# Loading and preparing the first pair's V ahead of the other pairs in a fused attention and mixer kernel

## The chip, the core and the metric

The kernel runs on one core of a Trainium2 chip. The metric is device time in microseconds (us). The engines are PE (TensorE, the matrix engine; PEld is its weight load), DVE (VectorE), ACT (ScalarE), POOL (GpSimd) and SP (SyncE, which here issues every DMA).

## The reference

```python
scores = scale * np.matmul(q, k.transpose(0, 1, 3, 2))     # batch 2, heads 12, seq 448, head_dim 64
scores = np.where(mask, -1000000000.0, scores)              # causal
attn = softmax(scores); x = np.matmul(attn, v)              # x: 2 x 448 x 768
xt = x.transpose(0, 2, 1)
u = x + (np.maximum(xt @ w_tok1, 0.0) @ w_tok2).transpose(0, 2, 1)   # token mixing, 448 -> 256 -> 448
y = u + np.maximum(u @ w_ch1, 0.0) @ w_ch2                  # channel mixing, 768 -> 1536 -> 768
h = gelu(y @ w_in)                                          # 768 -> 1024, halves u and v
gated = u * (w_sg applied over tokens to layernorm(v) + b_sg)
out = y + gated @ w_out                                     # 512 -> 768
```

The weights of the two mixing layers come as 64-bit floats. Products are kept near 32-bit accuracy by splitting each operand into a high and a low part and adding three matmuls.

## The kernel before

**Attention** runs over 24 heads in 12 pairs of two heads (`pair`, `order`). For a pair, `prep_qk` loads k (one DMA, 224 KB) and q (two DMAs), and `prep_v` loads V (one DMA, 320 KB, tile `vr`) and prepares it: the largest absolute value of each row on DVE (`am`, L255), a matmul that spreads it over the partitions (`vm`, L257), three short DVE operations that make the scale `sv` (L259 to L261), then the high half `vh` on ACT (L262) and the low half `vl` on DVE (L263). Each head has two halves, so a pair has four half-steps, 48 in all. A half-step (`probabilities`) makes scores on PE (L286, tile `s`), masks them and takes the row minimum on DVE (L291), takes the exponential on ACT (L298), rounds to a 16-bit high part on ACT (L300, `hl`), subtracts for the low part on POOL (L301) and transposes both parts with one DMA (L303, `pT<-hl`, "transpose" below; they are numbered 1 to 48 in order). `values` then multiplies the transposed probabilities with `vh` and `vl` on PE (L326 to L328, into `x_ps`, one buffer), and DVE scales the result of a pair (L342 to L344, `xf`). POOL and ACT split it into `xh` and `xl`.

**Token mixing** (`token_mix`) follows after every second pair: matmuls `a_ps` with w_tok1 (L361, L362, L136 to L138), a ReLU on ACT (`ah`, L366), matmuls `u_ps` with w_tok2 (L377) and the residual.

**Channel mixing** is the dense part: `channel_up` (`r_ps`, L136 to L138, 18 matmuls of 448 columns for one weight tile and one batch), then `channel_down` (`y_ps`). Each weight tile is loaded as 64-bit words (`wraw`, 768 KB, two buffers) and converted on ACT (`wm`, L113), DVE (L116, L117), ACT (`whi`, L121) and POOL (`wlo`, L94). Seven `channel_up` groups of the first batch (`NF0`, `up`) are written so that they may stand among the attention of the second batch. The gated layer (`v_ps`, `ug_ps`, `g_ps`, `o_ps`) ends the kernel.

**What sets the order.** The kernel is written in plain program order, and a scheduler that runs when the program is built orders the instructions of each engine, taking earlier written work first, unless a block gives another priority. `prepare_v` puts `prep_v` in such a block. On the chip each engine, and SP's queue of DMA issues, works through its own list in that fixed order. So a change of what is written first can move instructions anywhere in the attention.

Of the kernel before, what the change touches and what calls it, by code (L numbers as in the profile page):

```python
# [27 lines left out]
def mixer_kernel(  # L28
# [32 lines left out]
    AHEAD = 4  # L61
    VAHEAD = 2
# [133 lines left out]
    with ExitStack() as at:  # L196
# [42 lines left out]
        def prep_qk(b, n):  # L239

            qp = qps[n % len(qps)]
            k2 = qkp.tile([P, S], F32, tag="k2", name="k2")
            nc.sync.dma_start(k2, k[b, n])
            for i in range(2):
                nc.sync.dma_start(qp[i * D:(i + 1) * D, i * S:(i + 1) * S], q[b, n, i * D:(i + 1) * D])
            return qp, k2

        def prep_v(b, n):

            vr = qkp.tile([P, NVC, 2 * D], F32, tag="vr", name="vr", bufs=2)  # L250
            nc.sync.dma_start(vr, v[b, n])
            hi, lo = vts[n % NVT]
            vr4 = vr.rearrange("p c (h d) -> p c h d", h=2)
            am = stp.tile([P, 1], BF16, tag="am", name="am")
            nc.vector.tensor_reduce(am, vr[:, 1:5], AX.XY, ALU.max, apply_absolute_value=True)  # L255
            pm = ps_e.tile([P, 512], F32, tag="d", name="vm")
            nc.tensor.matmul(pm[:, :P], am.to_broadcast([P, P]), ident_b, start=True, stop=True)  # L257
            sv = stp.tile([P, 1], F32, tag="sv", name="sv")
            nc.vector.reduce_max(sv, pm[:, :P], axis=AX.X)  # L259
            nc.vector.tensor_scalar(sv, sv, 1e-20, 1.0 / VSCALE, ALU.max, ALU.mult)  # L260
            nc.vector.reciprocal(sv, sv)  # L261
            nc.scalar.activation(hi[:, :, :, :D], vr4, AF.Copy, scale=sv[:, 0:1])  # L262
            nc.vector.scalar_tensor_tensor(lo, vr4, sv[:, 0:1], hi[:, :, :, :D], ALU.mult, ALU.subtract)  # L263
            return hi, lo, sv
# [129 lines left out]
        qks, vss = {}, {}  # L394

        def prepare(n):
            if n < len(order):
                b, h = order[n]
                if h % 2 == 0:
                    qks[b, h // 2] = prep_qk(b, h // 2)  # L400

        def prepare_v(n):
            if n < len(order) and n % 2 == 0:
                b, h = order[n]

                with tc.high_priority(offset=-80):
                    vss[b, h // 2] = prep_v(b, h // 2)
# [6 lines left out]
            with tc.issue_after(marks[H - 2 + m]):  # L414
                channel_up(m, [0], rpool, ps_e)

        for n in range(AHEAD):
            prepare(n)
        for n in range(VAHEAD):
            prepare_v(n)  # L420
        for n, (b, h) in enumerate(order):
            prepare(n + AHEAD)
# [196 lines left out]
```

## Time and profile before

| | us |
|---|---|
| median of 3 runs | 428.05 (427.13 to 430.08) |
| the profiled execution's own time | 429.13 |
| its span, first to last instruction | 427.3 |
| PE busy in the span | 399.9 (94%) |
| PE idle in the span (the difference) | 27.4 |
[...]

The span is 1.8 us shorter than that execution's own time. Busy shares are averages over stages: attention ends near 170 us, and the dense part follows.

### The profile page before, as it was taken

To read this page: it belongs to the slowest core of one execution; us is meant where nothing else is said; L and a number is where in the kernel's file an instruction comes from. 1 tells how busy PE (TensorE), PEld (TensorE's weight loads), DVE (VectorE), ACT (ScalarE), POOL (GpSimd) and SP (SyncE) were. 2 spreads that over 40 slices of the span, in tenths; PEclk is the share of its full clock that TensorE was granted. 3 is DMA by queue.
4 is the path that set the end of the run, shared out by engine and by line. 5 is a ranking of instruction groups with operands and counts; after the bars stand their busy time and mean duration, and the time that the engine had idled before them with its cause. 6 is when DMAs were issued, how large, how long until landed. Compare 5 with 4: busy or idle time off the path is not lost.

```text
span 427.3 us, 6998 instructions
## 1 busy us (share of the span) xinstructions
PE 399.9 (94%) x2567; PEld 340.3 (80%) x2567; DVE 238.4 (56%) x522; ACT 204.2 (48%) x389; POOL 246.5 (58%) x234
## 2 busy tenths in 40 slices
PE   5878788888998999999999999999999999999996
PEld 3545666776787998999999999999998889965995
DVE  5989566787693645344444275557437451249422
ACT  3888678697665454445344244334423232332100
POOL 2789768769777564464335247454556653225662
PEclk9989999999898999999999999999999999999999
DMA  7999999999987854446344344453354001100122
GB/s 213 199 290 235 209 173 208 252 220 265 242 170 164 163 160 154 137 156 220 123 132 157 106 127 144 134 181 110 126 163 135 0 0 51 49 2 0 76 98 86
DMA packets 66738, 62.29 MB, mean 146 GB/s; under 512 B 53136, under 2 KB 58384, under 8 KB 66704
## 3 DMA queue, kind: packets, MB, share of 16 engines
q1 hardware_dynamic: 66704, 61.85, 56.5%
q8 instruction: 20, 0.33, 0.3%
q14 instruction: 14, 0.11, 0.1%
HBM read 46.50 MB, written 2.75 MB: 115 GB/s over the span
## 4 chain that ended last, share of the span: by engine, by line
PE 67%; DMA 12%; POOL 8%; ACT 5%; SPq 2%; issue 2%; DVE 2%; POOLq 0%; ACTq 0%; DVEq 0%
DMA pT<-hl 8%; PE y_ps L137 7%; PE y_ps L136 7%; PE y_ps L138 7%; PE r_ps L138 6%; PE r_ps L136 6%; PE r_ps L137 6%; POOL hl L301 4%; DMA vr<-in 2%; PE v_ps L138 2%; PE o_ps L136 2%; PE o_ps L138 2%; PE o_ps L137 2%; PE ug_ps L136 2%; PE v_ps L137 2%; PE ug_ps L138 2%
## 5 line engine op out<-in xcount | busy, mean ns | idle before, releaser
L94 POOL TENSOR_TENSOR wlo<-wm,whi 128x768 fp32r<-128x768 f32 (+1 forms) x41 | 81.3, 1984 | 75.6 <-ACT whi L121 75.1
L116 DVE TENSOR_SCALAR wm<-wm 128x768 int32<-128x768 int32 (+2 forms) x53 | 34.1, 643 | 88.0 <-ACT wm L113 88.0
L301 POOL TENSOR_TENSOR hl<-pe,hl 128x512 f16<-128x512 f32 x48 | 60.5, 1267 | 29.2 <-ACT hl L300 25.2
L113 ACT ACTIVATE wm<-wraw 128x768 f32<-128x768 f32 (+2 forms) x53 | 42.7, 805 | 59.1 <-POOL wlo L94 47.7
L286 PE MATMUL s_ps<-k,q 128*128 128x64 f32 (+3 forms) x216 | 57.9, 410 | 8.3 <-DMA q<-in 4.6
L138 PE MATMUL r_ps<-u_hi,wlo 128*128 128x448 f32 x144 | 53.4, 370 | 0.0
L137 PE MATMUL r_ps<-u_lo,whi 128*128 128x448 f32 x144 | 53.2, 369 | 0.0
L136 PE MATMUL r_ps<-u_hi,whi 128*128 128x448 f32 x144 | 53.1, 369 | 0.0
L136 PE MATMUL y_ps<-rh,whi 128*128 128x448 f32 x144 | 52.6, 365 | 0.0
L138 PE MATMUL y_ps<-rh,wlo 128*128 128x448 f32 x144 | 52.6, 365 | 0.0
L137 PE MATMUL y_ps<-rl,whi 128*128 128x448 f32 x144 | 52.6, 365 | 0.0
L121 ACT CAST whi<-wm 128x768 fp32r<-128x768 f32 (+1 forms) x41 | 32.8, 800 | 37.8 <-PE ug_ps L137 11.6
L117 DVE SCALAR_TENSOR_TENSOR wm<-wraw,wm 128x768 int32<-128x768 int32 (+2 forms) x53 | 50.1, 945 | 1.0
L286 PEld LDWEIGHTS s_ps<-k,q 128*128 128x128 f32 x216 | 32.4, 208 | 17.2 <-issue 6.6
L298 ACT ACTIVATE pe<-pe,bias 128x192 f32<-128x192 f32 (+3 forms) x84 | 40.2, 522 | 0.4
L291 DVE CUSTOM_DVE_ANT_0 pe<-s_ps,mask 128x320 f32<-128x320 f32 (+3 forms) x84 | 34.6, 444 | 7.9 <-PE s_ps L286 6.1
L300 ACT CAST hl<-pe 128x512 f16<-128x512 f32 x48 | 29.3, 612 | 18.3 <-DMA pT<-hl 17.9
L326 PE MATMUL x_ps<-vh,pT 128*128 128x65 f16 (+1 forms) x240 | 26.3, 197 | 11.6 <-DMA pT<-hl 10.9
L326 PEld LDWEIGHTS <-pT 128*128 128x128 f16 (+1 forms) x240 | 21.2, 98 | 19.6 <-DMA pT<-hl 14.6
L94 POOL TENSOR_TENSOR u_lo<-yt,u_hi 128x448 fp32r<-128x448 f32 x12 | 13.9, 1156 | 30.1 <-ACT u_hi L193 30.1
L138 PEld LDWEIGHTS r_ps<-u_hi,wlo 128*128 128x128 f32 x144 | 27.2, 189 | 2.6 <-issue 0.4
L136 PEld LDWEIGHTS r_ps<-u_hi,whi 128*128 128x128 f32 x144 | 27.3, 189 | 2.4 <-issue 0.2
(140 smaller groups left out, 918.7 us busy)
## 6 DMA issues: line engine op xcount, KB each, us to landing
wraw<-in SPq DMA_DIRECT2D x35, 768.0 KB, 4.5
wraw<-in SPq DMA_DIRECT2D x14, 512.0 KB, 3.9
vr<-in SPq DMA_DIRECT2D x12, 320.0 KB, 3.8
k<-in SPq DMA_DIRECT2D x12, 224.0 KB, 3.4
q<-in SPq DMA_DIRECT2D x24, 112.0 KB, 3.4
out<-ob SPq DMA_DIRECT2D x12, 224.0 KB, 1.9
wraw<-in SPq DMA_DIRECT2D x3, 256.0 KB, 3.1
pT<-hl SPq DMA_TRANSPOSE x48, 4.4
```

The costliest lines, as they stand in the source:

```text
L94: nc.gpsimd.tensor_sub(lo, src, f32(hi))
L113: nc.scalar.activation(m, words.bitcast(F32)[:, :, 1], AF.Prelu, scale=2.0 ** -112, alpha=-(2.0 ** 32))
L116: nc.vector.tensor_scalar(mi, mi, 3, None, ALU.logical_shift_left)
L117: nc.vector.scalar_tensor_tensor(mi, words[:, :, 0], 29, mi, ALU.logical_shift_right, ALU.bitwise_or)
L136: nc.tensor.matmul(ps, lh, rh, start=i == 0 and not begun, stop=False)
L137: nc.tensor.matmul(ps, lh, rl, start=False, stop=False)
L138: nc.tensor.matmul(ps, ll, rh, start=False, stop=i == n - 1)
L286: nc.tensor.matmul(ps[:, o:o + m], qp[:, q0:q0 + P], k2[:, ks], start=True, stop=True)
L291: nc.vector.tensor_tensor_reduce(out=pe[:, cs], in0=ps[:, cs], in1=mask0 if i == 0 else mask[:, MASKS[i]], scale=-1.0 / math.sqrt(D), scal ...
L298: nc.scalar.activation(pe[:, cs], pe[:, cs], AF.Exp, bias=bias[:, j:j + 1], scale=-1.0)
L301: nc.gpsimd.tensor_sub(hl[:, 1], pe, hl[:, 0])
L326: nc.tensor.matmul(o, ph, vh[:, c, h, :D + 1], start=j == 0, stop=False)
```

## The change

Before, the q and k of the first two pairs are requested first (`AHEAD` is 4 heads), and then the V of the first pair, in the block with the other priority. With the change the order is q and k of the first pair, V of the first pair, q and k of the second pair, and the first pair's `prep_v` is called directly, outside that block, before any scores are written. Nothing is added or taken away.

```diff
-        for n in range(AHEAD):
+
+        prepare(0)
+        vss[0, 0] = prep_v(0, 0)
+        for n in range(1, AHEAD):
             prepare(n)
-        for n in range(VAHEAD):
+        for n in range(1, VAHEAD):
             prepare_v(n)
```

Because the scheduler works from the program order, the lists of all engines differ through the whole attention. From the last token mixing on they are alike again. Three places:

**DVE at the start**, from the first score mask (`pe_194`) on. `am_163` before and `am_159` in the change are the first pair's V, `am_179` is the second pair's; `mx` rows belong to the mask above them. Before:

```order
L291 ISA pe_194,mx_195<-s_ps_193,mask0_76 128x64
L291 ISA mx_195 128x1
L291 ISA pe_194,mx_195<-s_ps_193,mask_77 128x448
L291 ISA mx_195 128x1
L291 ISA pe_228,mx_229<-s_ps_227,mask_77 128x192
L291 ISA mx_229 128x1
L291 ISA pe_228,mx_229<-s_ps_227,mask_77 128x320
L291 ISA mx_229 128x1
L255 TENSOR_REDUCE am_163<-vr_161 128x1
L291 ISA pe0_126,mx0_128<-s_ps_259,mask_77 128x448
L291 ISA mx0_128 128x1
L255 TENSOR_REDUCE am_179<-vr_177 128x1
```

With the change:

```order
L255 TENSOR_REDUCE am_159<-vr_157 128x1
L291 ISA pe_194,mx_195<-s_ps_193,mask0_76 128x64
L291 ISA mx_195 128x1
L291 ISA pe_194,mx_195<-s_ps_193,mask_77 128x448
L291 ISA mx_195 128x1
L291 ISA pe_228,mx_229<-s_ps_227,mask_77 128x192
L291 ISA mx_229 128x1
L291 ISA pe_228,mx_229<-s_ps_227,mask_77 128x320
L291 ISA mx_229 128x1
L259 TENSOR_REDUCE sv_163<-vm_161 128x1
L255 TENSOR_REDUCE am_179<-vr_177 128x1
L291 ISA pe0_126,mx0_128<-s_ps_259,mask_77 128x448
```

The first pair's `am` moves from behind four masks to ahead of the first, and the second pair's `am` from behind the mask of the third half-step (`pe0_126`) to ahead of it.

**SP's queue at the same time**; `pT_242`, `pT_268`, `pT_297` are transposes 2, 3 and 4, `vr_328` is the third pair's V, which reuses the first pair's `vr` buffer, and `wraw` is a token-mixing weight. Before:

```order
L303 DMA_TRANSPOSE pT_242<-hl_239 128x8x128
L105 DMA wraw_424<-in_3 128x256
L303 DMA_TRANSPOSE pT_268<-hl_265 128x8x128
L303 DMA_TRANSPOSE pT_297<-hl_294 128x8x128
L105 DMA wraw_432<-in_3 128x256
L251 DMA vr_328<-in_2 128x640
L243 DMA k2_574<-in_1 128x448
```

With the change:

```order
L303 DMA_TRANSPOSE pT_242<-hl_239 128x8x128
L105 DMA wraw_424<-in_3 128x256
L105 DMA wraw_432<-in_3 128x256
L245 DMA q1_135<-in_0 64x448
L251 DMA vr_328<-in_2 128x640
L303 DMA_TRANSPOSE pT_268<-hl_265 128x8x128
L243 DMA k2_574<-in_1 128x448
L303 DMA_TRANSPOSE pT_297<-hl_294 128x8x128
```

Transposes 3 and 4 stood ahead of `vr_328` and stand behind it now, and behind one more weight and a q load.

**SP's queue around transpose 41** (`pT_2012`); `pT_1873` and `pT_1902` are 39 and 40, and `wraw_2481`, `wraw_2514`, `wraw_2572` are the 6th, 7th and 8th channel-mixing weight tiles. Before:

```order
L105 DMA wraw_2481<-in_5 128x768
L303 DMA_TRANSPOSE pT_1873<-hl_1870 128x8x128
L303 DMA_TRANSPOSE pT_1902<-hl_1899 128x8x128
L105 DMA wraw_2514<-in_5 128x768
L105 DMA wraw_2572<-in_5 128x768
L303 DMA_TRANSPOSE pT_2012<-hl_2009 128x8x128
L303 DMA_TRANSPOSE pT_2047<-hl_2044 128x8x128
```

With the change:

```order
L105 DMA wraw_2481<-in_5 128x768
L303 DMA_TRANSPOSE pT_1812<-hl_1809 128x8x128
L105 DMA wraw_2514<-in_5 128x768
L303 DMA_TRANSPOSE pT_1847<-hl_1844 128x8x128
L303 DMA_TRANSPOSE pT_1873<-hl_1870 128x8x128
L303 DMA_TRANSPOSE pT_1902<-hl_1899 128x8x128
L105 DMA wraw_2572<-in_5 128x768
L303 DMA_TRANSPOSE pT_2012<-hl_2009 128x8x128
L303 DMA_TRANSPOSE pT_2047<-hl_2044 128x8x128
```

The 7th weight moves from behind transpose 40 to ahead of 38; the 8th still stands ahead of transpose 41. On DVE the last operation on the 6th weight, which frees the buffer that the 8th is loaded into, stood behind the first two masks of the last pair and stands ahead of them now; ACT's first operation on it stood behind the rounding of half-step 42 and stands behind that of 40 now.

**PE at the last token mixing**, from the last `a_ps` matmuls on. Before:

```order
L136 MATMUL a_ps_2294<-xh_1995,w1h_122 128x256
L137 MATMUL a_ps_2294<-xl_1996,w1h_122 128x256
L138 MATMUL a_ps_2294<-xh_1995,w1l_123 128x256
L377 MATMUL u_ps_2321<-w2h_124,ah_2317 128x448
L377 MATMUL u_ps_2321<-w2l_125,ah_2317 128x448
```

With the change:

```order
L136 MATMUL a_ps_2294<-xh_1995,w1h_122 128x256
L137 MATMUL a_ps_2294<-xl_1996,w1h_122 128x256
L138 MATMUL a_ps_2294<-xh_1995,w1l_123 128x256
L136 MATMUL r_ps_2522<-u_hi_84,whi_2512 128x448
L137 MATMUL r_ps_2522<-u_lo_85,whi_2512 128x448
```

Before, `u_ps` follows `a_ps` directly. Now one `channel_up` group of 18 `r_ps` matmuls stands between them. Over the attention, 47 `r_ps` matmuls stood on PE ahead of the second batch's second token mixing, and 33 do now; ahead of the last one there were 126 and are 108. The rest of the 432 follow it.

## Rows read from the trace of the kernel before

**Rows 1.** Windows: busy us (instructions) of PE, PEld, DVE, ACT, POOL; clock, DMA, GB/s.

```profile
0.00:11.00 11.00, 6.44 (x17) 4.39 (x18) 5.88 (x26) 4.12 (x8) 3.26 (x15) 1.00 0.73 213
11.00:45.00 34.00, 26.72 (x248) 17.07 (x247) 29.23 (x103) 27.27 (x69) 28.43 (x34) 0.95 1.10 237
45.00:109.00 64.00, 54.52 (x595) 43.00 (x596) 44.38 (x141) 49.97 (x114) 50.37 (x59) 0.98 1.08 223
109.00:130.00 21.00, 21.00 (x174) 18.27 (x175) 18.27 (x41) 14.34 (x29) 15.70 (x16) 0.98 0.86 189
130.00:135.00 5.00, 3.15 (x23) 2.35 (x22) 0.62 (x1) 3.75 (x10) 2.84 (x4) 0.87 1.11 209
135.00:160.00 25.00, 25.00 (x222) 23.03 (x222) 12.76 (x25) 13.57 (x23) 15.77 (x16) 0.96 0.66 164
160.00:170.00 10.00, 9.31 (x59) 8.42 (x58) 5.85 (x9) 4.58 (x7) 5.27 (x3) 1.00 0.43 160
170.00:410.00 240.00, 240.00 (x1172) 211.57 (x1171) 117.63 (x175) 86.58 (x130) 118.52 (x85) 1.00 0.33 105
```

**Rows 2.** What PE waited for, whole span: us in total, times, longest us.

```profile
PE x_ps L326 <- DMA pT<-hl: 10.9, 11, 2.3
PE s_ps L286 <- DMA q<-in: 4.6, 1, 4.6
...
PE a_ps L361 <- POOL xh L94: 2.1, 2, 1.8
...
PE u_ps L377 <- ACT ah L366: 0.7, 1, 0.7
```

**Rows 3.** DVE at the start: start us, us, what [idle before, releaser].

```profile
9.47 0.09 DVE L291 DVE_READ_ACCUMULATOR2_ANT mx<- 128x1 f32 x1
10.03 0.69 DVE L255 TENSOR_REDUCE am<-vr 128x1 bf16<-128x512 f32 x1 [0.48 <-DMA vr<-in]
10.63 0.61 DVE L291 CUSTOM_DVE_ANT_0 pe<-s_ps,mask 128x448 f32<-128x448 f32 x1
...
11.73 0.69 DVE L255 TENSOR_REDUCE am<-vr 128x1 bf16<-128x512 f32 x1 [0.47 <-DMA vr<-in]
...
18.20 1.10 DVE L263 SCALAR_TENSOR_TENSOR vl<-vr,sv,vh 128x640 f16<-128x640 f32 x1
```

**Rows 4.** SP's queue at the start.

```profile
2.39 0.59 SPq L243 DMA_DIRECT2D k<-in  x1
...
5.94 1.06 SPq L251 DMA_DIRECT2D vr<-in  x2
...
16.72 2.61 SPq L303 DMA_TRANSPOSE pT<-hl  x2
```

**Rows 5.** SP's queue around transposes 39 to 44.

```profile
112.29 4.58 SPq L303 DMA_TRANSPOSE pT<-hl  x2
117.04 6.79 SPq L105 DMA_DIRECT2D wraw<-in  x2
124.58 8.25 SPq L303 DMA_TRANSPOSE pT<-hl  x4
```

**Rows 6.** POOL: the low parts of half-steps 41 and 42.

```profile
113.97 2.58 POOL L301 TENSOR_TENSOR hl<-pe,hl 128x512 f16<-128x512 f32 x2 [1.16 <-ACT hl L300]
```

**Rows 7.** DVE: the last operation on the 6th channel-mixing weight.

```profile
121.38 2.06 DVE L117 SCALAR_TENSOR_TENSOR wm<-wraw,wm 128x768 int32<-128x768 int32 x1
```

**Rows 8.** ACT: the rounding of half-step 45.

```profile
131.25 0.62 ACT L300 CAST hl<-pe 128x512 f16<-128x512 f32 x1 [4.61 <-DMA pT<-hl]
```

**Rows 9.** Busy time in 100 us of `r_ps` and `y_ps` matmuls.

```profile
200.00:300.00 100.00, 100.00 (x495) 92.70 (x494) 52.05 (x68) 40.13 (x58) 46.20 (x28) 1.00 0.45 141
```

**Rows 10.** PE: first pair's last half-step of values, second pair's first.

```profile
21.92 0.20 PE L326 MATMUL x_ps<-vh,pT 128*128 128x65 f16 x1 [0.31 <-DMA pT<-hl]
...
26.81 0.23 PE L326 MATMUL x_ps<-vh,pT 128*64 128x65 f16 x2 [2.32 <-DMA pT<-hl]
```

## The prediction

> **What bounds the kernel.** I read the windows by stretch first. From 135 us to 410 us PE has next to no idle time: 25.00 of 25, 9.31 of 10 and 240 of 240 us [rows 1]. The matmuls do not change in number or shape, so the time can change only through PE's idle time and its clock. PE's idle time before 170 us is 4.56 us in the first stretch, 34 - 26.72 = 7.28, then 64 - 54.52 = 9.48, none from 109 to 130, 1.85 in 130 to 135, and 0.69 in 160 to 170: 23.9 us [rows 1]. The list of PE's waits puts names to the larger ones: 4.6 us for the first q, 10.9 us in 11 waits for a transpose, 2.1 us for `xh` ahead of token mixing, 0.7 us for `ah` [rows 2]. In the attention no compute engine is full, but the DMA share is 1.10 and 1.08 from 11 to 109 us [rows 1]: transposes, weights and q, k, V share engines that are always occupied. A transpose that SP issues late is therefore late for everyone behind it. From 109 us on, `channel_up` groups on PE cover most of this.
>
> **The start.** The first pair's V is requested at 2.39 us, where the second pair's k was, and not at 5.94 us [rows 4]. Its `am` then stands on DVE ahead of the first mask, and it can be done by about the time at which the first scores arrive; I count 0 to 0.3 us for that. The next `am`, the second pair's, is the costly one. Before, it came after the third half-step's mask and waited until 11.73 us for its data [rows 3]. The same bytes are ahead of it in SP's queue in both versions, so it lands near 11.7 us again, but now the mask of the third half-step stands behind it: DVE has nothing from 9.47 + 0.09 + about 0.3 us until 11.7, and that mask starts near 11.73 + 0.69 = 12.4 us, not at 10.63 [rows 3]. That is 1.8 us, with ACT's and POOL's work on the half-step queued behind it. `vl` gains its place ahead of three masks (some 1.5 us by the 0.61 us of one of 448 columns), and loses the 1.8 us: it starts at about 18.5 us, against 18.20 [rows 3]. It matters more what now waits for it. The third pair's V takes the first pair's buffer, so SP waits for `vl` before it issues that load, and transposes 3 and 4 are queued behind it. They went out from 16.72 us [rows 4]; with `vl` ending near 19.6 us they go out from about 20.2 us, **3.4 us later**. The first pair's values, whose last half-step ran at 21.92 us as soon as its transpose had landed [rows 10], end some 3.4 us later too. So the change does not bring the first pair forward: V was not what it waited for.
>
> Does that reach the end? The second pair's values waited 2.32 us for a transpose at 26.81 us [rows 10], and its transposes 5 and 6 now stand one behind the other with no load between them. What is late there is made up as long as DMA is always occupied: the same bytes are to be moved up to the point where `channel_up` begins, at a share of 1.10 and 1.08 [rows 1]. I take **0 us** from the start. The bounds are +3.4 us (all of the delay is kept) and -2 us (the earlier `vh` and `vl` take the wait of 2.32 us away).
>
> [...]
>
> **From 45 to 109 us** the lists differ everywhere, but nothing in the change aims there. I take 0, with 2 us to either side, about one of the longest waits for a transpose, 2.3 us [rows 2].
>
> **Transpose 41.** Here the new order removes a wait. Before, SP had transposes 39 and 40 out by 112.29 + 4.58 = 116.87 us, then went to the 7th and 8th weight tiles and sat on them from 117.04 to 123.83 us; transpose 41 went out at 124.58 [rows 5]. Its data was ready since 113.97 + 2.58 = 116.55 us at the latest [rows 6]. SP was held by the 8th weight, whose buffer came free only when DVE had finished the 6th, at 121.38 + 2.06 = 123.44 us [rows 7]. So transpose 41 lost 124.58 - 116.87 = 7.7 us. ACT waited 4.61 us for it before it could round half-step 45, at 131.25 us [rows 8]; POOL and the `xh` of token mixing stood behind that, and PE waited 1.85 us, its only idle time in 130 to 135 us [rows 1], of the 2.1 us for `xh` [rows 2]. In the change the 7th weight goes out before transpose 38, the 6th weight's turn on ACT comes two half-steps earlier, and on DVE it comes ahead of two masks. I expect 1 to 2 us of the 7.7 to be left, so `xh` some 6 us earlier.
>
> Against this stands what PE has to do meanwhile. Ahead of that token mixing there are now 33 `r_ps` matmuls, not 47. At 100 us for 495 [rows 9], 0.202 us each, PE gets there 14 x 0.202 = 2.8 us sooner. It had waited 1.85 us; with `xh` where it was, it would wait 1.85 + 2.8 = 4.65 us. With `xh` 6 us earlier it does not wait: **-1.85 us**. Bounds: +2.8 us, if `xh` is where it was, and -1.85, since no more than the whole wait can go.
>
> **The last token mixing.** PE waited 0.69 us for `ah` between the last `a_ps` and `u_ps` [rows 1, 2]. Now 18 `r_ps`, 3.6 us, stand between: **-0.69 us**. PE also reaches that token mixing 1.85 + 3.6 = 5.5 us sooner than before; what it needs there comes from transposes 45 to 48, which move up by about 6 us with transpose 41. I take no wait there; if there is one, it is the case just bounded.
>
> **Sum.** 0 + 0 - 1.85 - 0.69 = -2.54 us. The profiled execution took 429.13 us, so it would take 426.6; that execution is 1.1 us above the median of the runs. From the median of 428.05 the forecast is **425.5 us**, 0.6% less.
>
> **Rivals.** [...] (2) *Slower: the hold-up of SP's queue stays or moves.* The 8th weight still stands ahead of transpose 41, and the 7th now ahead of 38, so SP can wait for the same DVE and ACT operations two transposes earlier. Then `xh` comes no sooner, and the missing 14 matmuls are a hole: +2.8 - 0.69 = +2.1, 430.2 us. If `xh` comes g us sooner, PE's wait is 4.65 - g and the kernel changes by 2.8 - g - 0.69, so it turns slower where g falls below 2.1 us. With the whole delay of the start on top, +3.4, it is 433.6 us. (3) *Slower: the start's delay is kept* to the dense part, with transpose 41 freed: -2.54 + 3.4 = +0.9, 428.9 us. For it: transposes 3 and 4 are surely later. Against it: 9.48 us of idle PE time lies between [rows 1], in which a shift can be taken up. (4) *Nothing comes of it*: transpose 41 gains just what the missing matmuls use up, g = 2.8, and only the 0.69 is left: 427.4 us. The DMA share near 1 through the whole attention [rows 1] speaks for it, the 0.86 of 109 to 130 us against it.
>
> **How the numbers follow.** The forecast with its neighbourhood has 0.40, (1) 0.23, (2) 0.15 of which a third with the start's delay on top, (3) 0.12, (4) 0.10. A measurement of this kernel tells about 1%, 4.3 us, from no change. The forecast's -2.5 us is within that; (1) is mostly below 423.8, and some of the forecast's neighbourhood with its 2 us to either side is too: faster 0.26. Above 432.3 lie the worst of (2) and a tail of the stretches that I set to 0: slower 0.13. The rest, 0.61, is within 1%. The range goes from rival (1), 421.9, to a little above rival (2), 430.8 us.
>
> **What would show it.** In the profile of the changed kernel: DVE idle from about 9.9 us to the landing of the second V, and the third half-step's mask after 12 us; transposes 3 and 4 after 19 us; transpose 41 within 2 us of transpose 40's end and no gap of 6 us in SP's queue there; no PE wait for `xh` over 0.5 us in the second batch; no wait for `ah` at the end. The prediction is wrong if a wait of several us between 45 and 109 us appears or goes that I have no row for, or if PE sits idle between 109 and 135 us for want of the 14 matmuls.

## The result, and the profile after

The changed kernel takes 431.77 us (median of 20 runs, 428.68 to 434.73), the kernel before 428.74 us (20 runs, 425.24 to 432.80) in the same comparison: a ratio of 1.0087, 95% interval 1.0062 to 1.0112. It is slower by 0.9%, where I had 425.5 us, 0.6% faster, and it lies above my range. All ratios here and below leave out runs more than 1.5% above the fastest of their kernel, so some differ a little from that of the medians. The profiled execution took 429.86 us with a span of 428.1 us; it is one of the quicker ones, 1.9 us below its median, so its trace, 0.8 us longer than that of the kernel before, shows single waits better than their sum.

The windows of the changed kernel, in the stretches of [rows 1]:

```profile
0.00:11.00 11.00, 6.35 (x18) 4.08 (x19) 5.79 (x26) 4.12 (x8) 3.26 (x15) 1.00 0.78 208
11.00:45.00 34.00, 23.84 (x231) 15.06 (x229) 29.23 (x98) 26.16 (x66) 26.19 (x31) 0.99 1.03 230
45.00:109.00 64.00, 54.62 (x570) 43.65 (x570) 41.71 (x133) 48.21 (x109) 48.46 (x59) 0.93 1.07 226
109.00:130.00 21.00, 21.00 (x192) 17.40 (x191) 16.43 (x43) 15.71 (x35) 14.54 (x14) 0.91 0.88 200
130.00:135.00 5.00, 4.78 (x34) 3.90 (x33) 2.97 (x9) 4.26 (x11) 4.46 (x9) 1.00 0.83 161
135.00:160.00 25.00, 25.00 (x227) 22.82 (x227) 14.30 (x25) 12.76 (x23) 18.30 (x18) 1.00 0.62 143
160.00:170.00 10.00, 10.00 (x64) 9.52 (x63) 5.36 (x8) 5.84 (x9) 5.50 (x3) 1.00 0.51 170
```

The two gains of my sum are to be seen. From 130 to 135 us PE is busy for 4.78 us and not 3.15, from 160 to 170 us for 10.00 and not 9.31 [rows 1]: 1.63 and 0.69 us less idle time, where I had 1.85 and 0.69. But from 11 to 45 us, which I had set to 0, PE is busy for 23.84 us and not 26.72: 2.88 us more idle time. Not all of that is a loss, since the granted clock there was 0.99 and not 0.95, and matmuls took less time: those of the scores with 448 columns 566 ns on average (16), 617 before (18). PE's waits over the whole span, beside [rows 2], and under them the row of the kernel before that [rows 2] leaves out:

```profile
PE x_ps L326 <- DMA pT<-hl: 8.9, 9, 2.6
PE s_ps L286 <- DVE mx L291: 5.8, 9, 1.2
...
PE a_ps L361 <- POOL xh L94: 2.4, 1, 2.4
...
PE s_ps L286 <- DVE mx L291: 3.0, 4, 1.5
```

What grew is the second row: score matmuls that wait for a mask on DVE. Before, there were 3.0 us of it in 4 waits, now there are 5.8 in 9, and 4.7 of these in 8 lie between 11 and 45 us. Waits for transposes fell from 10.9 to 8.9 us. The wait for `ah` is gone; that for `xh` is 2.4 us in one and has another place (below).

The start, beside [rows 3] and [rows 4], by time: DVE first, then POOL, then SP's queue (transposes 3, 4, 9 and 12), then three of PE's waits for masks.

```profile
11.39 0.69 DVE L255 TENSOR_REDUCE am<-vr 128x1 bf16<-128x512 f32 x1 [1.54 <-DMA vr<-in]
12.00 0.61 DVE L291 CUSTOM_DVE_ANT_0 pe<-s_ps,mask 128x448 f32<-128x448 f32 x1
...
17.51 0.87 DVE L263 SCALAR_TENSOR_TENSOR vl<-vr,sv,vh 128x640 f16<-128x640 f32 x1
18.31 0.61 DVE L291 CUSTOM_DVE_ANT_0 pe<-s_ps,mask 128x448 f32<-128x448 f32 x1
...
18.85 0.35 DVE L291 CUSTOM_DVE_ANT_0 pe<-s_ps,mask 128x192 f32<-128x192 f32 x1
...
19.12 1.33 DVE L263 SCALAR_TENSOR_TENSOR vl<-vr,sv,vh 128x640 f16<-128x640 f32 x1
20.38 0.48 DVE L291 CUSTOM_DVE_ANT_0 pe<-s_ps,mask 128x320 f32<-128x320 f32 x1
...
17.68 0.97 POOL L119 TENSOR_SCALAR w1h<-wm 128x256 fp32r<-128x256 f32 x1 [1.26 <-DVE wm L117]
18.62 1.16 POOL L301 TENSOR_TENSOR hl<-pe,hl 128x512 f16<-128x512 f32 x1
...
19.80 1.24 SPq L303 DMA_TRANSPOSE pT<-hl  x1
...
22.20 1.25 SPq L303 DMA_TRANSPOSE pT<-hl  x1
...
34.07 2.43 SPq L303 DMA_TRANSPOSE pT<-hl  x1
...
43.50 1.99 SPq L303 DMA_TRANSPOSE pT<-hl  x1
...
15.92 1.02 PE L286 MATMUL s_ps<-k,q 128*128 128x448 f32 x2 [1.01 <-DVE mx L291]
...
21.01 1.98 PE L286 MATMUL s_ps<-k,q 128*128 128x128 f32 x8 [0.20 <-DVE mx L291]
...
39.71 1.25 PE L286 MATMUL s_ps<-k,q 128*128 128x128 f32 x6 [1.22 <-DVE mx L291]
```

DVE sits idle for 1.54 us until the data of the second `am` land, the mask of the third half-step starts at 12.00 us, transposes 3 and 4 go out at 19.80 and 22.20 us: near the times that I had given. What I had not read out of the order: the first `vl` at 17.51 and the second at 19.12 now stand ahead of masks of the seventh and eighth half-steps, which start at 18.31, 18.85 and 20.38 us. In the kernel before `vl` followed behind them [rows 3], and DVE had started them at 16.54, 17.51 and 17.79 us. On POOL the `hl` of the third half-step stands behind the second token weight, which waits 1.26 us for DVE; it starts at 18.62 us, and at 15.11 us before.

What is late there does not simply stay late. SP's queue before, transposes 9 and 12:

```profile
33.43 1.25 SPq L303 DMA_TRANSPOSE pT<-hl  x1
...
40.23 1.25 SPq L303 DMA_TRANSPOSE pT<-hl  x1
```

Transpose 4 is 4.1 us later than before, transpose 9 only 0.6 us, and transpose 12 again 3.3 us. At the end of the attention, when the same matmuls are done in both, the first `r_ps` behind the last token mixing starts at 169.8 us, at 169.0 before.

POOL's `hl` of half-step 37, SP's queue around transposes 37 to 47, beside [rows 5], and PE's one wait for `xh`:

```profile
111.30 1.47 POOL L301 TENSOR_TENSOR hl<-pe,hl 128x512 f16<-128x512 f32 x1
...
114.20 0.33 SPq L105 DMA_DIRECT2D wraw<-in  x1
114.64 1.23 SPq L303 DMA_TRANSPOSE pT<-hl  x1
117.57 0.33 SPq L105 DMA_DIRECT2D wraw<-in  x1
118.01 5.82 SPq L303 DMA_TRANSPOSE pT<-hl  x3
123.93 0.52 SPq L105 DMA_DIRECT2D wraw<-in  x1
126.87 15.25 SPq L303 DMA_TRANSPOSE pT<-hl  x7
...
106.48 0.58 PE L361 MATMUL a_ps<-xh,w1h 128*128 128x256 f32 x1 [2.39 <-POOL xh L94]
```

The long hold-up of SP ahead of transpose 41 (6.79 us at 117.04, [rows 5]) is gone, but that transpose goes out at 126.87 us, 2.3 us later than before. SP is held earlier instead: the 6th weight, which stood ahead of transpose 39, now stands ahead of 37 and gets its turn at 114.20 us, so transpose 37 goes out at 114.64 us, and at 105.31 before. The weight accounts for 1.9 us of that: the `hl` of half-step 37 is finished on POOL only at 111.30 + 1.47 = 112.77 us, at 103.07 before, behind token mixing's `xl` and a channel weight's `wlo`.

### The profile page after: what moved, and what is told of

Same layout as the page of the kernel before. It is cut to its first block, busy times and chain, and to the rows that moved or that the text cites. A ratio compares the mean times of both kernels' runs of the same rounds, so it can differ in the third digit from the quotient of the medians.

```text
span 428.1 us, 7002 instructions
## 1 busy us (share of the span) xinstructions
PE 400.1 (93%) x2567; PEld 340.9 (80%) x2567; DVE 238.5 (56%) x522; ACT 204.5 (48%) x389; POOL 245.6 (57%) x234
## 4 chain that ended last, share of the span: by engine, by line
PE 68%; POOL 3%; DMA 2%; issue 1%; ACT 1%; DVE 0%; POOLq 0%; ACTq 0%; DVEq 0%
PE y_ps L137 7%; PE y_ps L138 7%; PE y_ps L136 7%; PE r_ps L137 6%; PE r_ps L136 6%; PE r_ps L138 6%; PE v_ps L138 2%; PE o_ps L138 2%; PE o_ps L136 2%; PE o_ps L137 2%; PE v_ps L137 2%; PE ug_ps L136 2%; PE ug_ps L137 2%; PE ug_ps L138 2%; PE v_ps L136 2%; DMA pT<-hl 2%
## 5 line engine op out<-in xcount | busy, mean ns | idle before, releaser
L94 POOL TENSOR_TENSOR wlo<-wm,whi 128x768 fp32r<-128x768 f32 (+1 forms) x41 | 82.2, 2006 | 73.4 <-ACT whi L121 71.3
L116 DVE TENSOR_SCALAR wm<-wm 128x768 int32<-128x768 int32 (+2 forms) x53 | 35.0, 661 | 92.6 <-ACT wm L113 92.6
L301 POOL TENSOR_TENSOR hl<-pe,hl 128x512 f16<-128x512 f32 x48 | 58.9, 1237 | 26.9 <-ACT hl L300 25.8
L286 PE MATMUL s_ps<-k,q 128*128 128x64 f32 (+3 forms) x216 | 59.5, 418 | 10.5 <-DVE mx L291 5.8
L117 DVE SCALAR_TENSOR_TENSOR wm<-wraw,wm 128x768 int32<-128x768 int32 (+2 forms) x53 | 48.8, 922 | 1.1
L291 DVE CUSTOM_DVE_ANT_0 pe<-s_ps,mask 128x192 f32<-128x192 f32 (+3 forms) x84 | 34.5, 444 | 8.3 <-PE s_ps L286 7.0
L137 PEld LDWEIGHTS r_ps<-u_lo,whi 128*128 128x128 f32 x144 | 27.1, 188 | 2.4 <-issue 0.2
```

The lines of the kernel that those rows point to most:

```text
L94: nc.gpsimd.tensor_sub(lo, src, f32(hi))
L116: nc.vector.tensor_scalar(mi, mi, 3, None, ALU.logical_shift_left)
L117: nc.vector.scalar_tensor_tensor(mi, words[:, :, 0], 29, mi, ALU.logical_shift_right, ALU.bitwise_or)
L137: nc.tensor.matmul(ps, lh, rl, start=False, stop=False)
L286: nc.tensor.matmul(ps[:, o:o + m], qp[:, q0:q0 + P], k2[:, ks], start=True, stop=True)
L291: nc.vector.tensor_tensor_reduce(out=pe[:, cs], in0=ps[:, cs], in1=mask0 if i == 0 else mask[:, MASKS[i]], scale=-1.0 / math.sqrt(D), scal ...
```

## The experiments

**The theories.** S: the start's delay is kept to the end, and my two gains are real. O: the start is taken up, and the order that was derived anew for the rest of the attention costs. C: the granted clock, on average 0.982 in the profiled execution of the changed kernel and 0.988 in that of the kernel before, makes the difference. Later ones are named where they come up.

**How an order is held.** A scheduler derives the order of each engine anew for every edit, so that an edit in the source changes hundreds of places at once. To change one thing only, these kernels carry the whole order in a table, for all five engines, and a function that queues each instruction behind the one ahead of it in its row. The source is that of the kernel before; line numbers in these traces are 110 higher.

```diff
+def pin(tc, text):
+    import base64, json, zlib
+    ins = {i.name: i for i in tc.nc.cur_bb.bb.instructions}
+    for row in json.loads(zlib.decompress(base64.b85decode(text))):
+        for x, y in zip(row, row[1:]):
+            tc.add_manual_dep(
+                ins[f"I-{y}"], f"I-{x}",
+                mybir.DependencyInfo(mybir.DependencyClass.NoSync, mybir.DependencyReason.DATA), reason="pin",
+            )
...
         mixer_kernel(tc, *args)
+        pin(tc, ORDER)
```

A joined order is the first part of one kernel's and, behind it, what is left of the other's, in its order. Every kernel computes the whole reference.

| kernel | order | median us | ratio to before | 95% interval |
|---|---|---|---|---|
| start_after | changed to transpose 8, then before | 430.23 | 1.0041 | 1.0011 to 1.0071 |
| rest_after | before to transpose 8, then changed | 435.65 | 1.0120 | 1.0063 to 1.0177 |
| after_undo | changed, `am` and third V moved back | 432.79 | 1.0121 | 1.0082 to 1.0161 |
| before_delay | before, `am` and third V moved ahead | 429.65 | 1.0045 | 1.0010 to 1.0081 |
| rest11_after | before to transpose 11, then changed | 430.82 | 1.0059 | 1.0025 to 1.0092 |
| tail23_after | before to transpose 23, then changed | 432.68 | 1.0118 | 1.0075 to 1.0162 |
| head23_after | changed to transpose 23, then before | 433.59 | 1.0124 | 1.0083 to 1.0165 |
| after_fix4 | before to transpose 4, V early, then changed | 436.06 | 1.0176 | 1.0127 to 1.0225 |
| start13 | changed to transpose 13, then before | 433.54 | 1.0097 | 1.0060 to 1.0134 |
| rest13 | before to transpose 13, then changed | 429.07 | 1.0038 | 1.0009 to 1.0066 |
| tail34 | before to transpose 34, then changed | 429.36 | 1.0036 | 1.0007 to 1.0064 |
| head34 | changed to transpose 34, then before | 432.48 | 1.0107 | 1.0062 to 1.0153 |
| edit_only | before, the edit made by hand | 430.58 | 1.0061 | 1.0030 to 1.0093 |
| mix_S | start13 on SP alone | 438.03 | 1.0208 | 1.0161 to 1.0255 |
| mix_DP | start13 on DVE and PE alone | 442.27 | 1.0325 | 1.0287 to 1.0364 |
| mix_AL | start13 on ACT and POOL alone | 439.95 | 1.0290 | 1.0242 to 1.0337 |
| edit_late_v | edit_only, `vh` and `vl` moved back | 428.69 | 1.0020 | 0.9981 to 1.0059 |
| load_first | before, V's transfer moved alone | 426.81 | 0.9992 | 0.9957 to 1.0027 |

The kernel before ran beside each group, at medians of 427.4 to 428.3 us. The order written out costs nothing that shows: load_first, which has that of the kernel before but for one transfer, is at 0.9992.

**Two halves.** `cut(after, T8, before)` and `cut(before, T8, after)`, with

```
def cut(first, t, rest):
    k = first.index(t) + 1
    return first[:k] + [x for x in rest if x not in first[:k]]
```

start_after: 

> Each engine's order is written out: the changed kernel's up to transpose 8, then the order of the kernel before. Theory S (the start's delay is kept): second am ahead of the third half-step's mask, and the third pair's V ahead of transposes 3 and 4, delay these by 3 to 4 us, PE's idle time from 11 to 45 us is 2.9 us longer as in the changed kernel, and nothing takes it up; the wait for xh at 130 us stays. Time +2.9 us, ratio 1.007. Theory O (the order of the rest costs): the delay is taken up by 109 us, time as before, ratio 1.000. Theory C (the clock): the time follows the mean granted clock, 0.988 gives the time before and 0.980 gives 431.8 us, whichever half the kernel has.

rest_after: 

> The other half: the order of the kernel before up to transpose 8, then the changed kernel's. Theory S: transposes 3 and 4 go out near 16.7 us as before, the waits for xh at 130 us (1.6 us) and for ah at 165 us (0.7 us) are gone, time -2.3 us, ratio 0.995, as my prediction's sum had it. Theory O: +3 us, ratio 1.007, with new PE waits between 45 and 130 us. Theory C: as the mean granted clock says, 0.988 or 0.980.

The start costs 0.4%, 1.8 us, less than its 2.88 us of idle time; the rest, where my two gains are, costs 1.2% (from three runs) and gains nothing. Together the halves cost more than the whole, 1.6% against 0.9%, so something may be made at the joint.

**The two waits that I had named.** The order of the changed kernel with the second `am` and the third V moved back, and the order of the kernel before with the two moved ahead. Rows of after_undo against the changed kernel, DVE and SP:

```diff
-L365 TENSOR_REDUCE am<-vr 128x1
 L401 ISA pe_126,mx_128<-s_ps,mask 128x448
 L401 ISA mx_128 128x1
+L365 TENSOR_REDUCE am<-vr 128x1
...
-L361 DMA vr<-in 128x640
 L413 DMA_TRANSPOSE pT<-hl 128x8x128
 L353 DMA k_574<-in 128x448
 L413 DMA_TRANSPOSE pT<-hl 128x8x128
+L361 DMA vr<-in 128x640
```

after_undo: 

> The changed kernel's whole order, with two instructions moved: the second am on DVE behind the mask of the third half-step, and the third pair's V on SP behind transpose 4. Theory S: that mask near 10.7 us and not 12.0, transposes 3 and 4 near 17 us and not 19.8 and 22.2, PE's idle time from 11 to 45 us shorter by 2 to 3 us, and all of this reaches the end: 429 us or less, ratio to the kernel before 0.995 to 1.001, some 0.7% under the changed kernel's 1.0087. Theory O: the start is repaired in the same way, but the time stays at 431 to 432 us, ratio 1.007 to 1.009.

before_delay (the same two moves the other way, in the order of the kernel before): 

> The order of the kernel before, with two instructions moved: the second am on DVE ahead of the third half-step's mask, and the third pair's V on SP ahead of transpose 3; nothing else. This is the start's delay alone. Theory S: transposes 3 and 4 near 20 us, +2.9 to +3.4 us at the end, ratio 1.007 to 1.008. Theory O: transposes as late, but the time as before within 1 us, ratio 1.000 to 1.002. Theory C: as the mean granted clock says.

In after_undo the third half-step's mask is early again, and transpose 3 is as late as it was; DVE, POOL and SP:

```profile
10.25 0.62 DVE L401 CUSTOM_DVE_ANT_0 pe<-s_ps,mask 128x448 f32<-128x448 f32 x1 [0.34 <-PE s_ps L396]
...
17.53 0.97 POOL L229 TENSOR_SCALAR w1h<-wm 128x256 fp32r<-128x256 f32 x1 [1.26 <-DVE wm L227]
18.47 1.16 POOL L411 TENSOR_TENSOR hl<-pe,hl 128x512 f16<-128x512 f32 x1
...
19.65 1.24 SPq L413 DMA_TRANSPOSE pT<-hl  x1
```

The time is not better than the changed kernel's. So what held transpose 3 was not the second `am` and the third V, as I had said, but `hl` on POOL, behind the token weight that waits for DVE: it ends at 19.63 us. By itself, in before_delay, the delay of transposes 3 and 4 (to 21.1 us) costs 0.45%.

**Where the joint is.** Cuts at transposes 11 and 23, and the first 4 transposes as before with V early.

rest11_after: 

> The order of the kernel before up to transpose 11, then the changed kernel's. At this cut the two orders have issued the same instructions but for seven, at transpose 8 but for seventeen. Theory M (the middle): between the start and transpose 23 the changed order itself costs some 1%, and its end gives back 0.5%: ratio 1.004 to 1.006, the changed kernel's 1.0087 less the 0.0041 that its start alone cost. Theory J (the joint): the 1.2% of the cut at transpose 8 were made by the joint, where scores and values of the two orders do not fit; then this one is at 0.995 to 0.998.

tail23_after: 

> The order of the kernel before up to transpose 23, then the changed kernel's; the two have issued the same there but for six instructions. This holds the two terms of my sum and nothing else: transpose 41, and the r_ps ahead of the last u_ps. If the sum is right, no PE wait over 0.3 us for xh near 130 us and none for ah near 165 us, ratio 0.9945 (-2.3 us). Rival: what is saved there is given back between 95 and 125 us, where transpose 41 itself came 2.3 us later in the changed kernel than before; then ratio 0.999 to 1.002.

head23_after: 

> The other half of that: the changed order up to transpose 23, then the order of the kernel before. If start and middle cost what theory M says and the two terms at the end are worth 2.3 us, ratio 1.014; if the terms at the end are worth nothing, 1.009, as the whole change; if the cost is in the end and not in the middle, 1.004, as the start alone.

after_fix4 (in the old order up to transpose 4, V ahead of the second pair's k and q on SP, its `am` first on DVE, `vm` behind the fifth score matmul): 

> The changed kernel with the first pair's V loaded early as in the change, but the order of DVE, ACT, POOL, SP and PE up to transpose 4 that of the kernel before; behind it the changed order. On POOL the rounding residue hl of the third half-step again stands ahead of the token weights, which wait for DVE. Expected: transposes 3 and 4 near 17 us. Theory P (POOL's order is the start's delay, and it carries on): ratio 1.003 to 1.005. Rival (the delay of transposes 3 and 4 is not what costs): 1.008 to 1.012, as the changed kernel and the attempt with the second am and the third V.

These didn't settle it. In after_fix4 transposes 3 and 4 are as early as before (16.48 and 17.81 us) and the time is no better, but PE waits 7.4 us in 5 for an `am`, 1.8 in 3 in the changed kernel. In tail23_after PE waits 6.0 us in one, at 66 to 72 us, for the `am` of a V that the old order requests behind transpose 23 and the changed one behind 20: a joint that neither kernel has. So its 1.2%, and probably the 1.8% of after_fix4, say nothing of the change.

**Cuts without a joint.** Just behind transpose 13, the two orders have issued the same 512 instructions but for one q; around transpose 34 they differ by three of 1234.

start13: 

> The changed order up to transpose 13, then that of the kernel before. At this point the two have issued the same instructions but for one, so no joint is left that could cost. If the start costs what the cut at transpose 8 showed, 1.004; if also the hole at transposes 11 and 12, which went out 2.1 and 3.3 us later in the changed kernel, is kept, up to 1.008; if the start is taken up afterwards, 1.000.

rest13: 

> The order of the kernel before up to transpose 13, then the changed one. If the whole loss is in the start, the two terms of my sum are left, ratio 0.9945; if the middle costs too, 1.000 to 1.005. Above 1.006 the joints were not what made the earlier halves slow: then the changed order from transpose 13 on costs by itself.

tail34: 

> The order of the kernel before up to transpose 34, then the changed one, with three instructions of difference at the joint. It holds transpose 41 and the last token mixing alone, the two terms of my sum: ratio 0.9945 if they are worth 1.85 and 0.69 us, with no wait for xh near 130 us; 1.000 if they are taken up; over 1.003 if transposes 35 to 40 or the clock pay for them.

head34: 

> The changed order up to transpose 34, then that of the kernel before. If the two terms at the end are real, the changed kernel without them: 1.0087 + 0.0054 = 1.014. If they are worth nothing, 1.009. If the end is what costs, 1.004 or less.

With the changed order up to transpose 13 the kernel is 1.0% slower, with or without the changed middle (1.0097, 1.0107); with the old one it is at 1.004, again with or without it (1.0038, 1.0036). So the middle costs nothing that shows, the end brings nothing, and most of the 0.9% is the start: 1.0% where all else is old, 0.5% where all else is changed (1.0087 against 1.0038). The two parts add up to more than the whole, 1.35%, by about as much as their intervals allow. Up to transpose 8 the start cost 0.4%; what is added by transpose 13 may be the second delay, at transposes 11 and 12, which start13 has too (39.94 and 43.85 us, 37.59 and 40.23 before).

How start13 loses its 1.0% its trace does not show. The profiled execution is its quickest, 429.0 us with a median of 433.54, and in it the first `r_ps` behind the last token mixing starts at 168.9 us, no later than before.

What became of the end's gain show PE's waits from 95 to 175 us (total, times, longest) and SP's queue of tail34:

```profile
PE a_ps L471 <- POOL xh L204: 1.7, 2, 1.2
PE vm L367 <- DVE am L365: 1.5, 1, 1.5
PE a_ps L247 <- POOL xl L204: 0.4, 1, 0.4
...
126.26 16.27 SPq L413 DMA_TRANSPOSE pT<-hl  x7
```

The wait for `ah` is gone here too, but PE waits 1.7 us for `xh` and 1.5 us for an `am`: 3.6 us of waits, where the kernel before has 4.9 in that stretch. Transpose 41 goes out at 126.26 us.

**The edit by hand.** In the old order, only what the words of the change say, with `vl` ahead of three masks, as in the changed order, and `vh` ahead of the fifth half-step's exponentials. DVE, ACT, PE and SP against the kernel before, without the `mx` rows:

```diff
+L365 TENSOR_REDUCE am<-vr 128x1
 L401 ISA pe,mx<-s_ps,mask_76 128x64
...
-L365 TENSOR_REDUCE am<-vr 128x1
+L369 TENSOR_REDUCE sv<-vm 128x1
 L401 ISA pe_126,mx_128<-s_ps,mask 128x448
...
+L373 SCALAR_TENSOR_TENSOR vl_147<-vr,sv,vh_143 128x640
 L401 ISA pe_127,mx_129<-s_ps,mask 128x448
...
-L373 SCALAR_TENSOR_TENSOR vl_147<-vr,sv,vh_143 128x640
...
+L372 ACTIVATE vh_143<-vr,sv 128x10x64
 L408 ACTIVATE pe<-pe,bias 128x64
 L408 ACTIVATE pe<-pe,bias 128x448
 L406 ACTIVATE bias<-mx 128x2
-L372 ACTIVATE vh_143<-vr,sv 128x10x64
...
+L367 MATMUL vm<-ident_b,am 128x128
 L396 MATMUL s_ps<-k_153,q_134 128x448
...
+L361 DMA vr<-in 128x640
 L353 DMA k_157<-in 128x448
```

edit_only: 

> The order of the kernel before, with the edit made by hand and nothing else derived anew: on SP the first pair's V ahead of the second pair's k and q, on DVE its am ahead of the first mask, its sv behind the masks of the second half-step and vl one mask earlier, on ACT vh ahead of the fifth half-step's exponentials, on PE vm four score matmuls earlier. Theory E (the edit costs): ratio 1.006 to 1.010, with transposes 3 and 4 later than 19 us. Theory D (the order derived anew costs): transposes 3 and 4 at 16.5 to 17.5 us, ratio 0.997 to 1.003.

Theory D is wrong about the time and right about the transposes. The four go out as before (the last two at 16.61 us), and the kernel is 0.6% slower all the same. DVE, PE and SP, SP's one wait for PE ahead of a transpose from 14 to 30 us, and PE's window from 19 to 25 us (busy us, clock, DMA share, GB/s) here and in the kernel before:

```profile
17.13 1.37 DVE L373 SCALAR_TENSOR_TENSOR vl<-vr,sv,vh 128x640 f16<-128x640 f32 x1 [0.63 <-ACT vh L372]
18.42 0.61 DVE L401 CUSTOM_DVE_ANT_0 pe<-s_ps,mask 128x448 f32<-128x448 f32 x1
...
19.09 1.54 PE L396 MATMUL s_ps<-k,q 128*128 128x64 f32 x3 [1.85 <-DVE mx L401]
...
16.61 2.61 SPq L413 DMA_TRANSPOSE pT<-hl  x2
...
24.95 2.19 SPq L413 DMA_TRANSPOSE pT<-hl  x1
...
SPq L413 <- PE x_ps L438: 3.3, 1, 3.3
...
19.00:25.00 6.00, 5.91 (x34) 0.50 0.90 217
...
19.00:25.00 6.00, 5.02 (x73) 1.00 1.31 249
```

`vl`, three masks earlier and not one as I had expected, waits 0.63 us for `vh`, takes 1.37 us, and the mask of the seventh half-step behind it starts at 18.42 us and not at 16.54. PE, which has its scores in two buffers, waits 1.85 us for that mask. Transpose 5 goes out at 24.95 us, at 22.1 before. Its data are not what it waits for: its `hl` is finished at 21.39 us, earlier than before. SP waits 3.3 us for PE, since the transposed tiles have four buffers and the values of the first half-step must free one; their matmuls behind the first one start at 23.7 us, at 19.7 before. Of these 4.0 us the wait for the mask is a little under half. In the rest the clock shows: behind idle time from 17.2 us on it is 0.50 from 19 to 25 us, and six score matmuls take 2.29 us where they took 1.25 under 1.00, 1.04 us of the other 2.15. That it makes most of the rest is my estimate. In this execution the delay stays: transpose 13 at 47.5 us (43.5 before), the first `r_ps` behind the last token mixing at 171.0 us (169.0 before).

**The engines.** The first 512 instructions are those of both orders; one group of engines has them in the changed order, the others in the old one, and behind them all have the old one. DVE and PE wait for each other and can't be taken apart.

mix_S: 

> Up to transpose 13 SP has the changed order, that is all loads and transposes; the other engines have that of the kernel before, and behind transpose 13 all have. If the loads that now stand ahead of transposes 3, 11 and 12 are the cost, ratio 1.006 to 1.010, with transposes 11 and 12 two to three us later than 37.6 and 40.2; if not, 1.000 to 1.003.

mix_DP: 

> Up to transpose 13 DVE and PE have the changed order (they can't be had apart), ACT, POOL and SP that of the kernel before. PE's waits of score matmuls for masks were 1.5 us in 3 before, and 4.7 us in 8 in the changed kernel, up to 52 us. If they are the cost, they are here too and the ratio is 1.006 to 1.010; if not, 1.000 to 1.003.

mix_AL: 

> Up to transpose 13 ACT and POOL have the changed order, the others that of the kernel before. On POOL the third half-step's hl stands behind a token weight that waits for DVE, 18.62 us and not 15.11. If this is the cost, transposes 3 and 4 come 3 us later and the ratio is 1.006 to 1.010; if it is a delay that is taken up, 1.000 to 1.003. If all three groups are near 1.003, the loss is made by their meeting and has no one engine.

Each costs 2 to 3%, more than all together. Orders of single engines of this kernel do not fit together, so its start can't be split by engines to find the one that costs. This tells nothing of the change.

**The edit without its preparation.** Two moves taken back from edit_only, and V's transfer alone:

```diff
-L373 SCALAR_TENSOR_TENSOR vl_147<-vr,sv,vh_143 128x640
 L401 ISA pe_127,mx_129<-s_ps,mask 128x448
...
+L373 SCALAR_TENSOR_TENSOR vl_147<-vr,sv,vh_143 128x640
 L401 ISA pe,mx<-s_ps,mask_76 128x64
...
-L372 ACTIVATE vh_143<-vr,sv 128x10x64
 L408 ACTIVATE pe<-pe,bias 128x64
 L408 ACTIVATE pe<-pe,bias 128x448
 L406 ACTIVATE bias<-mx 128x2
+L372 ACTIVATE vh_143<-vr,sv 128x10x64
```

edit_late_v: 

> As the edit made by hand (ratio 1.0061), but vh on ACT and vl on DVE at their old places, behind the exponentials of the fifth half-step and behind three masks; V's transfer, am, vm and sv stay early. Theory V (vl and vh hold up masks and exponentials): PE's wait of 1.85 us for a mask at 19.1 us is gone, transpose 5 goes out near 22 us and not at 24.95, ratio 0.998 to 1.003. Rival (the second am, which keeps DVE for 1.35 us ahead of the masks of the fourth half-step, or the later k and q): ratio 1.005 to 1.008.

load_first (on SP, `vr` ahead of `k_157`, and nothing else): 

> The order of the kernel before with one instruction moved: the first pair's V goes out on SP ahead of the second pair's k and q. Nothing on the other engines is moved. If 320 KB ahead of the second pair's k and q delay its scores, PE waits for q or k near 10 us and the ratio is 1.003 to 1.006; if not, 0.999 to 1.002, and no wait for q but the first.

DVE of edit_late_v, by time:

```profile
16.36 0.60 DVE L401 CUSTOM_DVE_ANT_0 pe<-s_ps,mask 128x448 f32<-128x448 f32 x1
...
18.02 1.10 DVE L373 SCALAR_TENSOR_TENSOR vl<-vr,sv,vh 128x640 f16<-128x640 f32 x1
```

PE's wait for a q in load_first:

```profile
PE s_ps L396 <- DMA q<-in: 4.8, 1, 4.8
```

With `vl` behind the three masks again, transpose 5 goes out at 21.9 us, the wait of 1.85 us is gone, the clock from 19 to 25 us is 1.00, and the ratio is 1.002, not to be told from 1. The second `am` stands where it stood in edit_only. The early transfer alone costs nothing (0.9992), and PE's one wait for a q or k is the first, 4.8 us, as before. The second pair's k and q do land later, at 6.96, 7.26 and 8.09 us where they landed at 5.44, 5.98 and 6.85 before. That is 1.2 to 1.5 us, near the 1.4 us that 320 KB of V take at the 237 GB/s of the second stretch [rows 1] (an estimate), but no engine was waiting for these loads. No version here beats the kernel before beyond its interval.

## Why the prediction was wrong

**The step that failed** is "I take **0 us** from the start". The start costs 1.0% (start13), 4.2 us, with an interval of 2.6 to 5.7 us that holds my upper bound of 3.4; with all else changed it is 0.5%. My reason for 0 was that what is late there is made up as long as DMA is always occupied. It is made up for a while, as transpose 9 shows, but with DMA shares of 1.03 and 1.07 up to 109 us transpose 12 is 3.3 us late again, and the time of the runs does not come back. Of the 5.6 us between my -2.54 and the measured +3.0, 2.5 us are the two gains that did not come, and the other 3.0 about what the start costs.

**The reason inside it** was wrong as well. I had counted as a gain that `vl` stands "ahead of three masks". The masks lose what `vl` gains. In the old order that is probably the cost: PE's scores wait for the mask, the values come later, and the transpose that needs their buffer with them. edit_only and edit_late_v differ in `vh` and `vl` alone: means of 430.75 and 428.23 us in 12 runs each, 1.0061 and 1.0020. The traces show the wait of 1.85 us and the low clock behind it (0.50 against 1.00 from 19 to 25 us) in the one and not in the other, but the two intervals overlap. That it is also the cost in the changed kernel is not shown. There PE, behind the same two masks, waits 0.20 us at 21.01 us; its longer waits for masks are elsewhere, 1.01 us at 15.92 and 1.22 us at 39.71. I had also named the second `am` and the third V as what delays transposes 3 and 4. The times were nearly right (19.80 and 22.20 us against "from about 20.2"), by luck: the cause was another (after_undo), and `vl` had ended at 17.51 + 0.87 = 18.38 us, not near 19.6. Rival (3), "the start's delay is kept", comes nearest. I gave it 0.12 and 428.9 us, 2.9 us too little, since it kept my two gains at the end.

**Transpose 41**, "1 to 2 us of the 7.7 to be left, so `xh` some 6 us earlier": wrong. SP's hold-up moved to an earlier weight, as rival (2) has it (though to the 6th and not the 7th), and transpose 41 went out 2.3 us later. That transpose's own `hl` was finished at 123.00 us, at 115.43 before. PE's wait from 130 to 135 us went because PE came later: it begins that token mixing at 133.8 us, at 133.6 before, although 14 matmuls fewer stand ahead of it. It also waits 2.39 us for `xh` at the token mixing before that one, up to 106.48 us. Of the -1.85 nothing is left.

**The last token mixing**, -0.69 us: the wait is gone in the changed kernel and in tail34, as said. But tail34, which holds both terms, is at 1.0036. The terms that I could see were real idle time, and the kernel did not get shorter by them.

**Rival (1)**, the 421.9 us at the low end of my range, is the forecast less 1.65 us for the clock and 2 us from the start. No run shows either as time gained: the start costs 1.0% (start13). From 130 to 160 us, where the clock had been 0.87 and 0.96 [rows 1], it is 1.00 in the profiled execution of the changed kernel, 0.13 x 5 + 0.04 x 25 = 1.65 us by my estimate. But from 109 to 130 us it is 0.91 and not 0.98, by the same estimate 1.5 us of 21 the other way, and before that there is more of this (below).

**Right** were the late mask of the third half-step, the early transfer, for which the sum has nothing (load_first, 0.9992), and that the whole stays within 1%, the case that I gave 0.61.

**Open** is how the 1.0% of start13 divides and by which waits it reaches the end: the edit costs 0.6% in the old order, and whether the rest is the derived order or the uncertainty of both, the runs can't tell. Open is also the clock. The changed kernel's mean granted clock is 0.981 in its 20 runs, that of the kernel before 0.990 in the 108 that ran beside the experiments. Among the runs of one kernel, over all kernels, 0.01 less goes with 1.5 us more (290 runs, standard error 0.2). By that some 1.3 us of the difference would go with the clock. It is a correlation; whether the clock makes the time or PE's idle time makes both was not tried.

## What to carry to other kernels

An operation that is moved ahead pushes back what it is moved past: ask for each such operation who waits for what it delays, and follow the buffers too (in the hand-made edit: mask, score buffer, values, transposed tile, next transpose). Idle time on average does not show that a delay at the start will be taken up; a delay that shrinks can come back a few steps later (0.6 us at transpose 9, 3.3 us at transpose 12). So its bound is to be carried into the sum and not set to 0. Where a scheduler derives the order anew, write the order out and make the edit alone before crediting any stretch far from it. And join two orders only where both have issued the same instructions.

## What the hardware showed that I had not expected

The clock falls in the middle of the attention, and matmuls take longer there. PE of the changed kernel (busy us, clock, DMA share, GB/s):

```profile
40.00:45.00 5.00, 2.33 (x40) 0.94 1.02 259
45.00:50.00 5.00, 4.28 (x33) 0.50 1.20 210
50.00:55.00 5.00, 5.00 (x32) 0.87 0.82 166
```

From 40 to 45 us it was busy for 2.33 us of 5. In the next 5 us the clock is 0.50, and the matmuls there fill 4.28 us; PE is full in the 5 us after that. Busy time under 0.50 was less work done: a score matmul of 448 columns took 0.95 us at 47.52 us, and 0.54 us under 1.00 in the kernel before, at 12.10 us. By idle time 45 to 109 us is unchanged (54.52 and 54.62 us busy), while the clock went from 0.98 to 0.93, by my estimate up to 0.05 x 64 = 3.2 us under 1.00. In other stretches it rose, as from 11 to 45 us, 0.95 to 0.99. A sum of idle times misses both.

The 1.00 from 0 to 11 us, before and after, does not fit what PE did. A score matmul of 448 columns takes 0.95 us there in the kernel before (at 9.28 us) and 0.90 us in the changed kernel (at 9.59 us), near the 0.95 us under 0.50 and far from the 0.54 us at 12.10 us. So the first scores were about as slow as scores under 0.50 in both.
